# Attention and two expert layers on one core: attention in pairs, one-bank PSUM tiles, another order

## The chip, the cores and the metric

The kernel runs on one core of a Trainium2 chip. The metric is the device time of one execution in microseconds (us), lower is better. The engines are TensorE (PE, with its weight loads as PEld), VectorE (DVE), ScalarE (ACT), GpSimd (POOL) and SyncE (SP), which issues nearly all DMAs.

## What is computed

Attention with memory slots and a local window, then a relu-squared layer of two matrix products, then a gated one:

```python
def _attn_ref(q, k, v, mem_k, mem_v):
    ...
    for c in range(nc):
        ...
        scores = scale * np.matmul(q_c, k_full.transpose(0, 1, 3, 2))
        scores = scores - np.max(scores, axis=-1, keepdims=True)
        a = np.exp(scores)
        a = a / (np.sum(a, axis=-1, keepdims=True) + 1e-09)
        out[:, :, c_start:c_end] = np.matmul(a, v_full)

def _moe_ref(x, w_in, w_out, s, b):
    r = np.maximum(x @ w_in, 0.0)
    return (s * (r * r) + b) @ w_out

def _moe2_ref(x, w_in, w_out):
    h = x @ w_in
    return (h * (1.0 / (1.0 + np.exp(-1.702 * h)))) @ w_out
```

Attention has 4 x 8 heads of 768 positions and 64 columns, in chunks of 32 with 64 keys each (8 of memory, 56 of the window). Its output, 3072 tokens x 512, goes through both layers, whose inner width is 2048.

## The kernel before, in words

**Attention** runs over 24 tiles of 128 tokens (`attend`). For each tile the queries and keys are loaded; PE makes the scores `sc` (L454) as a block of 64 small matmuls of 64x32 by 64x64; DVE takes the maximum and subtracts it (L471, L474); ACT does the exponential; PE transposes the result (`pp`, L487), ACT or DVE copies it to `px`; PE multiplies by the values (`o`, L515, again 64 small matmuls); DVE divides by the sums (L520); PE transposes back (`xx`, L529), and copies and a subtraction split the result into a high and a low part, `xh` and `xl`. Tiles 0 to 3 are parts of their own, and from 4 on two tiles make a part (`parts`); in such a pair, scores, `pp`, `o` and `xx` share a PSUM tile of two banks with the tag "a", or "accA" for those in `SIDE`.

**The products** are made in three passes each: high by high, high by low, low by high. Four of the six blocks of 512 tokens of the first layer go straight: `ph` (L644) in a PSUM bank, the gate on ACT and DVE, then the sums `accA` and `accB` (L677), of four banks in all. The other two blocks, and all of the second layer, go by seven products instead of eight (a Strassen-Winograd scheme, function `wino`, four rounds `s` of eight pairs `p` each). Seven inner products of the first matrix, called A, B, C and D in two parts each (`product`, L1015 to L1017), are summed in the PSUM tiles `ph`, `pb`, `pc` and `pd`. A is copied by ACT into the bank of B, and B into the bank of C (`seed`, L1059), before B's and C's own matmuls begin there. Gates follow (L1027, the first use of another function needs an ACT_TABLE_LOAD), then the splits `oj` and `oq` of their results (L1137, L1140) and seven outer products (`outer_product`, L1166 and L1172), whose results are added and stored by `away` (L1194, L1201). The last one ends with two adds of 512 columns and two stores.

**What sets the order.** Nothing is scheduled by hand: each piece of work is an `op` of the class `Plan`, with the engines that can do it and a planned duration, the ops and buffers that it needs, and a time `need`. `Plan.order` walks a model of the engines and chooses, by a due time `late` that it derives from `need`, which op each engine takes next; a gap `AFTER` is added when another engine has to hear of it. The program is emitted in that order, and each engine runs its own list in order, waiting on semaphores. Ops marked dense are the attention blocks (`sc`, `o`); `SPACE` keeps two of them at least 2.4 us apart. Where PE is planned to be idle for over 0.3 us, filler matmuls `idle` (L1304) on a constant tile `cold` are put in; eight `warm` ones (L301) begin the program.

**PSUM.** `ps_acc` holds the sums, `ps_h` two banks of `ph`, `ps_a` the two banks of attention. `pair` gives the two-bank tiles: a `Banks` of two one-bank tiles for "accB", one tile of two banks for "accA" and "a". Waits between engines are made for tiles.

Of the kernel before, what the change touches and what calls it, by code (L numbers as in the profile page):

```python
# [8 lines left out]
F32 = mybir.dt.float32  # L9
# [23 lines left out]
WARM = 8  # L33
# [12 lines left out]
S_PE = 0.8  # L46
V_PE = 0.8

class Plan:
# [30 lines left out]
    def order(self):  # L80
# [20 lines left out]
        for i in range(len(ops) - 1, -1, -1):  # L101
# [7 lines left out]
            late[i] = self.due.get(i, min(due))  # L109

# [7 lines left out]
        holds, packed = {}, [-9.0]  # L118
# [25 lines left out]
        while left:  # L144
# [29 lines left out]
            if i in self.dense:  # L174
                packed[0] = t
# [40 lines left out]
def attention_moe_moe(ctx: ExitStack, tc: tile.TileContext, q_t, k_w, v_w, w_in1, w_out1, s_b, w_in2, w_out2, out):  # L216
# [13 lines left out]
    ps_a = ctx.enter_context(tc.tile_pool(name="ps_a", bufs=1, space=PS))  # L230
# [55 lines left out]
    def chill(e):  # L286
        cold = pp.tile([P, KT, 512], F32, tag="ys", name="cold")
        T["cold"] = cold[:, 1].bitcast(F32R)
        fill(e, cold[:, 0], 0.0)
        nc.vector.tensor_copy(out=T["cold"], in_=cold[:, 0])  # L290

    plan.tag("r", 1)
    o_cold = op(-999, {"dve": 0.7}, chill, alloc=[("ys", "cold")])
    plan.due[o_cold] = -1000.0
    o_ident = op(-135, {"pool": 0.5}, lambda e: make_identity(nc, ident))
# [8 lines left out]
    op(-999, {"pe": 0.46 * WARM}, warm, after=[o_cold], alloc=[("h", "warm")], uses=["cold"])  # L304


    managers = {"gp": pool_g, "att": pool_a}
# [115 lines left out]
    def bank(name, u):  # L423
        T[name, u] = (ps_acc if u in SIDE else ps_a).tile([P, 2, 512], F32, tag="accA" if u in SIDE else "a", name=name)
        return T[name, u]

    def attend(u):
# [168 lines left out]
        for i in ids if b > 3 else ():  # L596
            z = op(px + 1, {"act": 0.6, "dve": 0.5}, whole(i), after=[bk[i]], uses=[("xx", u), ("px", g)])
            o_xd.append(op(px + 1, {"sp": 0.8}, away(i), after=[z], uses=[("px", g)]))
        for i in ids if b < 4 else ():
            nth = u[i] % 4  # L600
            first = [o_x[u[i] - nth][0]] if nth else []
            z = op(px + 1, {"act": 0.6, "dve": 0.69}, keep(i), after=[bk[i]] + first,
# [10 lines left out]
    def pair(tag, name):  # L613
        if tag == "accB":
# [748 lines left out]
```

## Time and profile before

| | |
|---|---|
| median of 3 runs | 1084.7 us (1083.78 to 1085.21) |
| profiled execution | 1084.78 us, span 1083.0 us |
| PE busy | 1063.8 us, 98% |
| DVE busy | 763.4 us, 70% |
| ACT busy | 598.5 us, 55% |
| TensorE clock granted, mean | 0.998 of full speed |
| DMA | 265.68 MB, mean 245 GB/s |

The span runs from the first to the last instruction on the core; the time of the execution is 1.8 us longer. Busy time is time in which the engine works on something; matmuls overlap, so the time between two starts tells more than a duration. A bracket at the end of a timeline row is the idle time ahead of it and what ended it.

### The profile page before, as it was taken

What the parts mean: (1) busy time and instruction counts of PE and PEld (TensorE: products, weight loads), DVE (VectorE), ACT (ScalarE), POOL (GpSimd) and SP (SyncE); (2) the same over time, 40 slices, a digit from 0 to 9 for tenths busy, and PEclk for the clock granted to TensorE, in tenths of its full rate; (3) what the DMA queues carried; (4) which work ended last, traced back from release to release, by engine and by line L of the source; (5) the groups of instructions that cost most, each with busy time, mean ns of one, the idle gap of its engine ahead of it and who ended that gap; (6) DMA issues with size and microseconds to landing.
All of it is one profiled execution on the core that took longest, in us unless ns stands there. A gap on an engine that the chain in (4) does not pass through costs nothing.

```text
span 1083.0 us, 21691 instructions
## 1 busy us (share of the span) xinstructions
PE 1063.8 (98%) x8588; PEld 908.4 (84%) x8588; DVE 763.4 (70%) x1155; ACT 598.5 (55%) x921; POOL 0.7 (0%) x6
## 2 busy tenths in 40 slices
PE   8899999999999999999999999999999999999998
PEld 6777887778877788788888777999888999888998
DVE  7898986778798658888999554995223985222944
ACT  5668755545666647688744665543355532454432
POOL 0000000000000000000000000000000000000000
PEclk9999999999999999999999999999999999999999
DMA  9988934658699964888978998867656766666662
GB/s 341 313 279 295 304 125 142 229 180 304 212 328 313 371 222 152 308 298 271 326 225 282 340 346 283 262 203 252 195 185 212 235 196 221 193 187 205 196 204 79
DMA packets 151541, 265.68 MB, mean 245 GB/s; under 512 B 14224, under 2 KB 65424, under 8 KB 151440
## 3 DMA queue, kind: packets, MB, share of 16 engines
q1 hardware_dynamic: 151152, 263.77, 72.9%
q8 instruction: 68, 1.11, 0.4%
q10 hardware_dynamic: 288, 0.52, 0.1%
q14 instruction: 33, 0.27, 0.1%
HBM read 190.84 MB, written 73.40 MB: 244 GB/s over the span
## 4 chain that ended last, share of the span: by engine, by line
PE 88%; DMA 2%; ACT 2%; DVE 0%; SPq 0%; issue 0%; DVEq 0%
PE ph L644 14%; PE pc L1166 10%; PE accA L677 7%; PE accB L677 7%; PE pd L1166 6%; PE pb L1166 6%; PE pc L1172 3%; PE pd L1015 3%; PE pd L1017 3%; PE pd L1016 3%; PE ph L1015 3%; PE ph L1017 3%; PE ph L1016 3%; PE pc L1015 2%; PE pc L1017 2%; PE pc L1016 2%
## 5 line engine op out<-in xcount | busy, mean ns | idle before, releaser
L1140 DVE TENSOR_TENSOR oj<-G,oj 128x1024 fp32r<-128x1024 f32 x72 | 87.9, 1222 | 51.3 <-ACT oj L1137 50.8
L1137 ACT CAST oj<-G 128x1024 fp32r<-128x1024 f32 x72 | 75.6, 1051 | 87.5 <-PE pd L1166 28.6
L650 ACT ACTIVATE r<-ph 128x512 f32<-128x512 f32 (+1 forms) x66 | 38.5, 583 | 75.3 <-PE ph L644 68.8
L1137 ACT CAST oq<-G 128x1024 fp32r<-128x1024 f32 x40 | 42.1, 1052 | 51.6 <-PE pc L1166 22.0
L1140 DVE TENSOR_TENSOR oq<-G,oq 128x1024 fp32r<-128x1024 f32 x40 | 48.9, 1222 | 27.3 <-ACT oq L1137 27.3
L1166 PE MATMUL pc<-wih,oj 128*128 128x256 f32 x336 | 62.4, 284 | 0.0
L665 ACT CAST gh<-r 128x512 fp32r<-128x512 f32 (+1 forms) x66 | 40.0, 606 | 37.4 <-PE accB L677 34.9
L1149 DVE TENSOR_TENSOR G<-G 128x1024 f32<-128x1024 f32 x48 | 57.2, 1220 | 0.4
L669 DVE TENSOR_TENSOR gl<-r,gh 128x512 fp32r<-128x512 f32 (+1 forms) x66 | 44.1, 668 | 17.3 <-ACT gh L665 16.7
L368 ACT ACTIVATE u<-st 128x512 f32<-128x512 f32 x64 | 42.6, 670 | 22.8 <-DMA st<-w_in 12.9
L1027 ACT ACTIVATE G<-ys 128x512 f32<-128x512 f32 x64 | 40.6, 634 | 24.9 <-DVE ys L1069 24.4
L1166 PE MATMUL pd<-wih,oj 128*128 128x256 f32 x288 | 53.8, 284 | 0.0
L1166 PEld LDWEIGHTS pc<-wih,oj 128*128 128x128 f32 x336 | 53.3, 192 | 0.0
L1166 PE MATMUL pc<-wil,oj 128*128 128x256 f32 x168 | 47.6, 284 | 0.0
L1166 PEld LDWEIGHTS pd<-wih,oj 128*128 128x128 f32 x288 | 45.9, 192 | 0.0
L1166 PE MATMUL pc<-wih,oq 128*128 128x256 f32 x240 | 45.7, 284 | 0.0
L380 DVE SCALAR_TENSOR_TENSOR u<-u,st 128x512 uint32<-128x512 uint32 x64 | 43.4, 685 | 2.4 <-ACT st L376 1.4
L1166 PE MATMUL pb<-wih,oj 128*128 128x256 f32 x240 | 44.7, 284 | 0.0
L386 DVE SCALAR_TENSOR_TENSOR u<-st,u 128x512 uint32<-128x512 uint32 x64 | 43.5, 686 | 0.5
L376 ACT ACTIVATE st<-st 128x512 uint32<-128x512 uint32 x64 | 42.9, 672 | 0.8 <-DMA st<-w_out 0.7
L657 ACT ACTIVATE r<-r 128x512 f32<-128x512 f32 (+1 forms) x66 | 40.8, 618 | 1.6
L677 PE MATMUL accA<-gh,woh 128*128 128x512 f32 (+1 forms) x132 | 41.5, 390 | 0.0
(253 smaller groups left out, 3011.0 us busy)
## 6 DMA issues: line engine op xcount, KB each, us to landing
wih<-wodh SPq DMA_DIRECT2D x112, 256.0 KB, 2.9
wil<-wodl SPq DMA_DIRECT2D x112, 256.0 KB, 3.4
wih<-wch SPq DMA_DIRECT2D x96, 256.0 KB, 3.5
wil<-wcl SPq DMA_DIRECT2D x96, 256.0 KB, 3.9
st<-w_in SPq DMA_DIRECT2D x32, 512.0 KB, 6.5
st<-w_out SPq DMA_DIRECT2D x32, 512.0 KB, 6.0
k<-k_w SPq DMA_DIRECT2D x24, 512.0 KB, 5.4
v<-v_w SPq DMA_DIRECT2D x24, 512.0 KB, 5.9
```

The costliest lines, as they stand in the source:

```text
L380: nc.vector.scalar_tensor_tensor(out=u, in0=u, scalar=3, in1=T["st", i][:, :, 0], op0=ALU.logical_shift_left, op1=ALU.bitwise_or)
L386: nc.vector.scalar_tensor_tensor(out=u, in0=T["st", i][:, :, 1], scalar=0x80000000, in1=u, op0=ALU.bitwise_and, op1=ALU.bitwise_or)
L644: nc.tensor.matmul(T["ph", i], T[win][x][:, k * P:(k + 1) * P], T["x", m, b][y][:, k, r], start=seen_["hid"] == 1, stop=seen_["hid"] == 3 ...
L669: nc.vector.tensor_tensor(out=gl, in0=T["r", i], in1=gh.bitcast(F32), op=ALU.subtract)
L677: nc.tensor.matmul(T["acc", group, k // 2][:, k % 2][:, r], T[wout][x][:, k * P:k * P + P], T["g", i][y], start=fresh and (x, y) == (0, 0) ...
L1015: nc.tensor.matmul(ph, wh, xh, start=first and i == 0, stop=False, skip_group_check=True)
L1016: nc.tensor.matmul(ph, wh, xl, start=False, stop=False, skip_group_check=True)
L1017: nc.tensor.matmul(ph, wl, xh, start=False, stop=i == 1, skip_group_check=True)
L1137: nc.scalar.copy(out=T[kh], in_=g_of(ty, z))
L1140: nc.vector.tensor_tensor(out=T[kl], in0=g_of(ty, z), in1=T[kh].bitcast(F32), op=ALU.subtract)
L1149: o_raw[out, x] = [op(need, {"dve": 1.22}, lambda e: nc.vector.tensor_tensor(out=g_of(out, z), in0=g_of(a, z), in1=g_of(b, z), op=o), afte ...
L1166: nc.tensor.matmul(a, lt[:, z], rh, start=first and t % 2 == 0 and x == 0, stop=p == HALF - 1 and x == 2, skip_group_check=True)
```

## The change

- **Pairs and form.** The planner no longer keeps dense blocks apart (`SPACE` is gone). It counts 0.09 us for going into the form of the attention blocks and 0.25 for going out of it, so two blocks can stand one directly behind the other. The copies behind transposes wait for all transposes of the pair. Planned durations are set anew (`S_PE`, `V_PE`, `AFTER`, copies, gates).
- **One bank for each PSUM tile.** `pair` gives two one-bank tiles everywhere. Attention has its own two-bank tiles in `ps_x` (tiles of `SIDE`) and `ps_a`; these pools are handed over to `ps_y` and `ps_b` for the sums and the seven products when attention is through with them.
- **Table of shifts.** `SHIFTS`, some 250 entries (first op, number of ops, us), is added to the due times.
- **Start.** `cold` is a memset without a cast; the table of Exp is loaded by an op of its own (`table`); nine warm matmuls.
- **End.** The last outer product of the last round is cut in two halves, one for each bank, and `last` adds and stores bank 1 in two halves of 256 columns and bank 0 in one piece.

```diff
-WARM = 8
+WARM = 9
...
-S_PE = 0.8
-V_PE = 0.8
+S_PE = 0.66
+V_PE = 0.66
+
+SHIFTS = (
+    (3509, 64, 0.24), (1579, 256, -5.54), (408, 256, -2.04), (2922, 1, 0.96), (1298, 16, 5), (690, 1, 18.27),
...
-    AFTER = {"pe": 0.2, "act": 0.05, "dve": 0.05, "pool": 0.2, "sp": 0.1, "aq": 0.1, "none": 0.0}
+    AFTER = {"pe": 0.2, "act": 0.035, "dve": 0.035, "pool": 0.2, "sp": 0.1, "aq": 0.1, "none": 0.0}
...
-    BEAT = 0.24
-    SPACE = 2.4
+    BEAT, COLD, SLOW = 0.24, 6.5, 0.45
+    INTO, OUT_OF = 0.09, 0.25
...
+        shift = [0.0] * len(ops)
+        for at, n, by in SHIFTS:
+            for i in range(at, min(at + n, len(ops))):
+                shift[i] += by
+        late = [x + y for x, y in zip(late, shift)]
...
-            if i in self.dense:
-                t = max(t, packed[0] + self.SPACE)
+            if e == "pe" and (i in self.dense) != packed[0]:
+                t += self.OUT_OF if packed[0] else self.INTO
...
-                if idle > 0.3:
-                    full.append((None, int((idle - 0.3) / self.BEAT)))
+                if clock and idle > 0.3:
+                    full.append((None, int((idle - 0.3) / (self.SLOW if clock < self.COLD else self.BEAT))))
...
-        T[name, u] = (ps_acc if u in SIDE else ps_a).tile([P, 2, 512], F32, tag="accA" if u in SIDE else "a", name=name)
+        T[name, u] = (ps_x if u in SIDE else ps_a).tile([P, 2, 512], F32, tag="s", name=name)
...
-            tc_.append(op(pv, {"act": 0.48, "dve": 0.6}, turned(i), after=[tt[i]], uses=[("pp", u)], **fresh("px")))
+        for i in ids:
+            tc_.append(op(pv, {"act": 0.59, "dve": 0.69}, turned(i), after=list(tt), uses=[("pp", u)], **fresh("px")))
...
     def pair(tag, name):
-        if tag == "accB":
-            return Banks([ps_acc.tile([P, 512], F32, tag=f"{tag}{n}", name=name) for n in range(2)])
-        return (ps_a if tag == "a" else ps_acc).tile([P, 2, 512], F32, tag=tag, name=name)
+        pool = {"accB": ps_acc, "accA": pools.get("ps_y"), "a": pools.get("ps_b")}[tag]
+        return Banks([pool.tile([P, 512], F32, tag=f"{tag}{n}", name=name) for n in range(2)])
...
-            return op(need, {"pe": 1.36}, fn, after=after + ready[x] + [o_in[p, n]],
+            return op(need, {"pe": 1.38}, fn, after=after + ready[x] + [o_in[p, n]] + o_late,
...
+        def last(n, b, part, need, after, end):
+            held = ("turn", s) + BANKS[n]
+            lo, hi = (part, part + 1) if b else (0, 2)
+            z = slice(256 * lo, 256 * hi)
+
+            def fn(e):
+                nc.vector.tensor_tensor(out=spot(b)[:, z], in0=T[held][:, b][:, z], in1=spot(b)[:, z], op=ALU.add)
...
+            d = op(need, {"dve": 0.42 if b else 0.69}, fn, after=[end] + after, uses=[tmp, held])
+            o = op(need, {"sp": 0.37 if b else 0.73}, store, after=[d], uses=[tmp])
...
+                    if s == len(SEVEN) - 1 and n == 2 and p == HALF - 1:
+                        prev = [outer_product(n, p, here + 8 * p + only, key, d, prev + wait, only) for only in range(2)]
...
+    def swap(e):
+        follow("att", "late", bufs=1, side="right")(e)
+        follow("ps_a", "ps_b", bufs=1, space=PS, side="right")(e)
+
+    o_late = [op(-1, {"none": 0.0}, swap, after=stage_ops)]
```

Three places of PE's list show what moves. In these rows the number behind a name tells tiles apart, and `32x64 x32` is one attention block. The first is the startup, tiles 2 and 3; before:

```order
L454 MATMUL sc_506<-k_272,qe_352 32x64 x32
L487 MATMUL pp_546<-ident_137,qe_352 128x128 x4
L1304 MATMUL idle_155<-cold_149 128x512
L515 MATMUL o_565<-v_396,px_556 32x64 x32
L1304 MATMUL idle_155<-cold_149 128x512 x2
L529 MATMUL xx_610<-ident_137,px_556 128x128 x4
L487 MATMUL pp_620<-ident_137,qe_352 128x128 x4
L1304 MATMUL idle_155<-cold_149 128x512 x2
L515 MATMUL o_638<-v_396,px_556 32x64 x32
L1304 MATMUL idle_155<-cold_149 128x512 x2
L529 MATMUL xx_680<-ident_137,px_556 128x128 x4
L1304 MATMUL idle_155<-cold_149 128x512 x2
```

In the change:

```order
L511 MATMUL sc_444<-k_267,qe_340 32x64 x32
L511 MATMUL sc_480<-k_267,qe_340 32x64 x32
L701 MATMUL ph_434<-xl0_401,wih_425 128x256 x4
L701 MATMUL ph_434<-xh0_400,wil_426 128x256 x4
L1393 MATMUL idle_183<-cold_152 128x512 x3
L544 MATMUL pp_544<-ident_140,qe_340 128x128 x4
L544 MATMUL pp_558<-ident_140,qe_340 128x128 x4
L1393 MATMUL idle_183<-cold_152 128x512
L572 MATMUL o_570<-v_382,px_563 32x64 x32
L572 MATMUL o_608<-v_382,px_563 32x64 x32
L1393 MATMUL idle_183<-cold_152 128x512
L586 MATMUL xx_650<-ident_140,px_563 128x128 x4
```

The two tiles ran one behind the other from the transposes on, and now run step by step together.

The second is a pair of tiles in the middle of attention, among the sums of the first layer; before:

```order
L677 MATMUL accB_2609<-gh_2930,wol_1952 128x512
L454 MATMUL sc_3018<-k_2744,qe_2811 32x64 x32
L644 MATMUL ph_3054<-xh1_2585,wih_421 128x512 x4
L644 MATMUL ph_3054<-xl1_2586,wih_421 128x512 x4
L454 MATMUL sc_3018<-k_2744,qe_2811 32x64 x32
L644 MATMUL ph_3054<-xh1_2585,wil_422 128x512 x4
L677 MATMUL accA_2605<-gh_2984,woh_2010 128x512
```

In the change (the scores of the same pair, tiles 12 and 13):

```order
L734 MATMUL accB_2602<-gh_2889,wol_1953 128x512
L734 MATMUL accB_2603<-gh_2889,wol_1953 128x512
L511 MATMUL sc_2995<-k_2725,qe_2790 32x64 x64
L734 MATMUL accA_2598<-gh_2943,woh_2035 128x512
L734 MATMUL accA_2599<-gh_2943,woh_2035 128x512
```

The two blocks of scores had eight expert matmuls of 512 columns between them, and now stand directly behind one another (`x64`).

The third is the second round of seven products, sixth pair; `pc_7481` is the two-bank tile of B and D before, `pd_7464` is one bank of C. Before:

```order
L1015 MATMUL pc_7481<-xl1_6294,wih_7427 128x512
L1016 MATMUL pc_7481<-xl1_6294,wih_7427 128x512
L1017 MATMUL pc_7481<-xl1_6294,wil_7428 128x512
L1015 MATMUL pc_7481<-xl0_6398,wih_7423 128x512
L1016 MATMUL pc_7481<-xl0_6398,wih_7423 128x512
L1017 MATMUL pc_7481<-xl0_6398,wil_7424 128x512
L1015 MATMUL pc_7481<-xl0_6398,wih_7423 128x512
L1016 MATMUL pc_7481<-xl0_6398,wih_7423 128x512
L1017 MATMUL pc_7481<-xl0_6398,wil_7424 128x512
L1015 MATMUL pd_7464<-xh0_6397,wih_7427 128x512
L1016 MATMUL pd_7464<-xh0_6397,wih_7427 128x512
L1017 MATMUL pd_7464<-xh0_6397,wil_7428 128x512
```

In the change (`pc_7524` is the bank of B, `pc_7525` that of D):

```order
L1072 MATMUL pc_7525<-xl0_6356,wih_7433 128x512
L1073 MATMUL pc_7525<-xl0_6356,wih_7433 128x512
L1074 MATMUL pc_7525<-xl0_6356,wil_7434 128x512
L1072 MATMUL pc_7524<-xl1_6307,wih_7438 128x512
L1073 MATMUL pc_7524<-xl1_6307,wih_7438 128x512
L1074 MATMUL pc_7524<-xl1_6307,wil_7439 128x512
L1072 MATMUL pc_7524<-xl1_6307,wih_7438 128x512
L1073 MATMUL pc_7524<-xl1_6307,wih_7438 128x512
L1074 MATMUL pc_7524<-xl1_6307,wil_7439 128x512
L1072 MATMUL pd_7501<-xs_6322,wih_7374 128x512
L1073 MATMUL pd_7501<-xs_6322,wih_7374 128x512
L1074 MATMUL pd_7501<-xs_6322,wil_7375 128x512
```

Before, six D matmuls stood between the last of B and the first of C, which needs the copy of B; now D stands ahead of B, and a second part of A (on `xs`) behind it.

## Rows read from the trace of the kernel before

**Rows 1.** Page, part 1: busy us of each engine (share), instructions
```profile
PE 1063.8 (98%) x8588; PEld 908.4 (84%) x8588; DVE 763.4 (70%) x1155; ACT 598.5 (55%) x921; POOL 0.7 (0%) x6
```

**Rows 2.** Windows: length; busy PE, PEld, DVE, ACT, POOL; PEclk, DMA share, GB/s
```profile
0.00:37.00 37.00, 29.55 (x612) 22.02 (x613) 26.50 (x54) 19.99 (x36) 0.70 (x6) 0.95 0.92 332
37.00:100.00 63.00, 62.32 (x797) 50.87 (x797) 56.55 (x99) 46.43 (x81) 0.00 (x0) 1.00 0.91 303
100.00:400.00 300.00, 297.60 (x3278) 239.61 (x3277) 234.94 (x408) 175.94 (x277) 0.00 (x0) 1.00 0.72 245
400.00:700.00 300.00, 296.03 (x1364) 245.51 (x1363) 239.05 (x368) 194.52 (x310) 0.00 (x0) 1.00 0.83 284
700.00:1078.30 378.30, 378.30 (x2543) 350.40 (x2541) 205.07 (x227) 161.60 (x220) 0.00 (x0) 1.00 0.63 198
```

**Rows 3.** PE groups by form: busy us, mean ns, idle before
```profile
L454 PE MATMUL sc<-k,qe 64*32 64x64 f32 x1536 | 20.6, 224 | 0.1
...
L1304 PE MATMUL idle<-cold 128*128 128x512 f32 x35 | 13.2, 479 | 3.6 <-DVE cold L290 1.9 <-issue 1.7
```

**Rows 4.** PE timeline around two attention blocks: start us, us, operation
```profile
234.53 0.62 PE L677 MATMUL accA<-gh,wol 128*128 128x512 f32 x2
234.98 0.62 PE L677 MATMUL accB<-gh,wol 128*128 128x512 f32 x2
235.53 0.86 PE L454 MATMUL sc<-k,qe 64*32 64x64 f32 x64
236.31 1.21 PE L644 MATMUL ph<-xh,wih 128*128 128x512 f32 x4
237.36 1.09 PE L644 MATMUL ph<-xl,wih 128*128 128x512 f32 x4
238.38 0.86 PE L454 MATMUL sc<-k,qe 64*32 64x64 f32 x64
```

**Rows 5.** PE timeline of the startup, tiles 2 and 3
```profile
21.87 0.86 PE L454 MATMUL sc<-k,qe 64*32 64x64 f32 x64
...
24.04 0.86 PE L454 MATMUL sc<-k,qe 64*32 64x64 f32 x64
...
26.75 0.34 PE L515 MATMUL o<-v,px 64*32 64x64 f32 x12 [0.44 <-ACT px L249]
28.94 0.75 PE L515 MATMUL o<-v,px 64*32 64x64 f32 x52 [1.85 <-issue]
...
33.28 0.98 PE L515 MATMUL o<-v,px 64*32 64x64 f32 x64
...
36.80 0.62 PE L644 MATMUL ph<-xh,wih 128*128 128x256 f32 x3 [0.20 <-ACT xh L249]
```

**Rows 6.** The same view, 30 to 34 us
```profile
30.00:34.00 4.00, 3.86 (x73) 2.82 (x74) 3.24 (x8) 1.71 (x3) 0.00 (x0) 0.57 0.77 274
```

**Rows 7.** Timeline of the end, DVE
```profile
1078.38 1.29 DVE L1194 TENSOR_TENSOR ys<-pc,ys 128x512 f32<-128x512 f32 x2 [6.45 <-PE pc L1166]
```

**Rows 8.** PE's waits, 37 to 400: us in total, times, longest
```profile
PE xx L529 <- DVE px L520: 1.1, 1, 1.1
PE o L515 <- ACT px L249: 1.0, 4, 0.2
```

**Rows 9.** PE's waits, 400 to the end
```profile
PE pd L1015 <- ACT pd L1059: 1.3, 2, 0.7
PE pc L1015 <- ACT pc L1059: 1.2, 1, 1.2
```

**Rows 10.** ACT timeline at two seed copies
```profile
606.29 1.28 ACT L1027 ACT_TABLE_LOAD   x1
...
657.39 0.57 ACT L1059 COPY pd<-pc 128x512 f32<-128x512 f32 x1 [1.09 <-PE pc L1017]
```

**Rows 11.** PE timeline at the same two places
```profile
610.76 0.50 PE L1015 MATMUL pc<-xl,wih 128*128 128x512 f32 x1 [1.18 <-ACT pc L1059]
...
658.02 0.50 PE L1015 MATMUL pd<-xh,wih 128*128 128x512 f32 x1 [0.66 <-ACT pd L1059]
```

More of the change, by code (lines that the diff above doesn't have):

```diff
@@ L286, in chill, with table @@
     def chill(e):
[L287 to L290, printed above, removed]
+        T["cold"] = pp.tile([P, KT, 512], F32, tag="ys", name="cold")[:, 0].bitcast(F32R)
+        fill(e, T["cold"].bitcast(F32), 0.0)
+    def table(e):
+        x = const.tile([P, 1], F32, name="one")
+        nc.scalar.activation(out=x, in_=T["cold"].bitcast(F32)[:, :1], func=AF.Exp)
     plan.tag("r", 1)
-    o_cold = op(-999, {"dve": 0.7}, chill, alloc=[("ys", "cold")])
+    o_cold = op(-999, {"dve": 0.6}, chill, alloc=[("ys", "cold")])
     plan.due[o_cold] = -1000.0
+    plan.due[op(-999, {"act": 1.5}, table, after=[o_cold], uses=["cold"])] = -1000.0
     o_ident = op(-135, {"pool": 0.5}, lambda e: make_identity(nc, ident))
@@ L303, in attention_moe_moe @@
     plan.tag("h", 2)
[L304 to L307 removed]
+    op(-999, {"pe": 0.43 * WARM}, warm, after=[o_cold], alloc=[("h", "warm")], uses=["cold"])
+    managers = {"gp": pool_g, "att": pool_a, "ps_x": pool_x, "ps_a": pool_p}
     def follow(old, new, **kw):
@@ L601, in attend @@
             first = [o_x[u[i] - nth][0]] if nth else []
-            z = op(px + 1, {"act": 0.6, "dve": 0.69}, keep(i), after=[bk[i]] + first,
+            z = op(px + 1, {"act": 0.6, "dve": 0.69}, keep(i), after=bk + first,
                    alloc=[] if nth else [(f"x{HOME[b]}", ("x", 0, b))], uses=[("xx", u)])
@@ L1046, in gates @@
                 b = op(need, {"act": 0.62, "dve": 0.69}, square, after=[b])
-                b = op(need, {"act": 0.73, "dve": 0.54}, affine, after=[b])
+                b = op(need, {"act": 0.815, "dve": 0.54}, affine, after=[b])
             o_g[ty, p] = b
@@ L1150, in sums, with outer_product @@
                 out=g_of(out, z), in0=g_of(a, z), in1=g_of(b, z), op=o), after=after + o_raw[a, x] + o_raw[b, x])]
-        def outer_product(n, p, need, key, d, after):
+        def outer_product(n, p, need, key, d, after, only=None):
             tag, turn = BANKS[n]
@@ L1161, in fn @@
                 if m:
-                    for t in range(4):
+                    for t in range(4) if only is None else range(2 * only, 2 * only + 2):
                         z = slice(t * P, t * P + P)
@@ L1173, in fn @@
                                              stop=p == HALF - 1 and x == 2, skip_group_check=True)
-            return op(need, {"pe": 1.45 if m else 1.36}, fn, after=o_part[n, p // 2] + [d] + after, alloc=taken(tag, held),
+            return op(need, {"pe": 0.72 if only is not None else 1.44 if m else 1.36}, fn, after=o_part[n, p // 2] + [d] + after, alloc=taken(tag, held),
                       uses=[("wp", s, n, p // 2), key + ("h",), key + ("l",), held])
@@ L1254, in wino @@
                 elif n == 2:
-                    away(n, b, b, e, [got["u4", b], got["c22", b]], False, False, b)
+                    if s == len(SEVEN) - 1:
+                        for part in range(b + 1):
+                            last(n, b, part, e, [got["u4", b], got["c22", b]], o_end[n][b])
+                    else:
+                        away(n, b, b, e, [got["u4", b], got["c22", b]], False, False, b)
         for x in range(HALF // 2):
@@ L1258, in wino @@
             free_g[3, x], free_g[1, x] = o_part[5, x] + o_raw[2, x], o_part[2, x]
+    side_ops = []
     for u in parts:
         if u[0] < 8:
+            one = len(plan.ops)
             attend(u)
+            if u in SIDE:
+                side_ops.extend(range(one, len(plan.ops)))
+    o_y_pool = [op(-1, {"none": 0.0}, follow("ps_x", "ps_y", bufs=1, space=PS), after=side_ops)]
     for i in range(2 * NF):
@@ L1279, in attention_moe_moe @@
             attend(u)
-    o_late = [op(-1, {"none": 0.0}, follow("att", "late", bufs=1, side="right"), after=stage_ops)]
+    def swap(e):
+        follow("att", "late", bufs=1, side="right")(e)
+        follow("ps_a", "ps_b", bufs=1, space=PS, side="right")(e)
+    o_late = [op(-1, {"none": 0.0}, swap, after=stage_ops)]
     wo_ops = []
```

30 lines of the change are left out of this document (20 added, 10 removed), and 41 rows, old and new, of the table SHIFTS.

## The prediction, on record before the change was run

> **What bounds the kernel now.** I read the totals first, then idle time by stretch, then the stretches one by one. PE is busy for 1063.8 of 1083.0 us [rows 1], so only two things can shorten the kernel: PE's 19.2 us of idle time, and work that PE does not have to do. By stretch the idle time is 7.45 us before 37 us, 0.68 + 2.40 = 3.08 us in the rest of attention, 3.97 us in 400 to 700, and nothing from 700 to PE's end, where PE is busy 378.30 of 378.30 [rows 2]. The remaining 4.7 us lie at the end. Busy time hides two more losses: 35 fillers of the line `idle` [rows 3], which PE runs where it would wait, and the price of changing form between dense attention blocks and ordinary matmuls. All sums below start from the profiled execution, 1084.78 us, which is 0.1 above the median of the runs.
>
> **Joined attention blocks.** One tile's `sc` or `o` is a block of 64 matmuls on 64x32. The block is 0.86 us long and one matmul 0.224 [rows 3, 4], so 63 starts take 0.86 - 0.224 = 0.64 us, 10 ns each. What a block costs is read from its neighbours. Two 128x512 matmuls take 0.45 (234.53 to 234.98), but the two before the block need 0.55, 0.10 more. The block holds PE for 0.78 (235.53 to 236.31), 0.14 more than its starts. The four matmuls behind it need 1.05 where 4 x 0.227 = 0.91 is due, 0.14 more [rows 4]. Together 0.10 + 0.78 + 0.14 = 1.02 us, of which 0.38 is the change of form there and back. A second block directly behind the first pays only its 0.64 or 0.65, and saves 0.36 to 0.38; I take 0.36. The order of the change has 25 runs of such blocks where the kernel before has 48, so 23 blocks are joined: 20 after the first expert work of tiles 2 and 3, and 3 in the startup, which is counted next. 20 x 0.36 = **7.2 us**. The block is on PE, which bounds, so the gain is all on the path. Bounds: 0 (two tiles change the PSUM address and weights, and no row shows two tiles back to back), and 20 x 0.49 = 9.8, if the 0.11 us by which the next four matmuls (237.36 to 238.38) are over their 0.91 too is a late part of leaving this block, and not the way into the next.
>
> **Startup.** The first `ph` of tiles 2 and 3 comes at 36.80 us [rows 5]. Their chain is `sc` of tile 3 at 24.04, softmax, transposes, `o` of tile 2 at 26.75, which stops after 12 matmuls and goes on at 28.94 with 1.85 us put down to "issue", then `o` of tile 3 only at 33.28, since the two tiles run one behind the other [rows 5]. Between 30 and 34 the granted clock is 0.57, most of it at the lower of the two levels, 1.2 GHz, right behind that hole; it costs (1 - 0.57) x 4 = 1.7 us [rows 6]. The change runs the two tiles, which stay parts of their own with a PSUM tile each, step by step together: `sc` twice in a row, four transposes twice, `o` twice. I work its chain from the same rows. `sc` of tile 2 to its own `o` takes 26.75 - 21.87 = 4.9 now. Together they add the second `sc` (0.64), two more DVE operations (1.29 for two on 128x512 [rows 7]) and four more transposes, about 0.44: 7.3, so `o` at 21.9 + 7.3 = 29.2. From `o` of tile 3 to `ph` it is 36.80 - 33.28 = 3.5 now; with the second `o` 4.1, so `ph` at 33.3. What the second tile adds to that tail on DVE (0.65) and in transposes (0.44) I set against the hole and the queues inside the two stretches, which the two now pass once. Nothing covers the 0.44 here: they are in the 7.3. Against 36.80 the gain is **3.5 us**. Bounds: 0 (the fetch of instructions stalls again, and DVE work of the experts stands between the steps) to 5 (the 1.85 and the 1.7 both go, and 1.4 of queues).
>
> **Waits in the rest of attention.** The 3.08 us consist of `xx` waiting for DVE's normalizing (1.1, one time), `o` waiting for ACT's copies (1.0, four times) and smaller ones [rows 8]. Each also lengthens the first matmul behind it by some 0.11 us (worked out with the next part), so that 8 of them make 4.0. The planner's corrected durations (the copy of a transpose at 0.59 instead of 0.48 on ACT) are those errors which let it place `o` too early. From tile 4 on the copies now wait for all eight transposes of a pair, 0.44 us later for the first; expert matmuls lie in between there and cover it, and without them it would cost 0.44 twice in each of 10 pairs. I take **2.5 us**, bounds -1 and 4.
>
> **Seven products.** The idle time of 400 to 700 is products waiting for seed copies on ACT, `pd` twice and `pc` once among them [rows 9]. Two causes can be seen. At 606.29 an ACT_TABLE_LOAD of 1.28 us stands in ACT's queue ahead of the seed, and PE waits 1.18 us until 610.76 [rows 10, 11]. At 657.39 the copy `pd<-pc` starts 1.09 us after its engine came free, released by PE, and PE then waits 0.66 until 658.02 [rows 10, 11]. The copy reads the bank of product B, but the six D matmuls on the other bank come between (6 x 0.227 = 1.4 us; the order in the part on the change shows them), and B and D are one two-bank tile: the copy waits for the last matmul of both. What the row shows is a wait that is one product too long. The Trainium skill, "PSUM — Partial Sum Buffer", section "PSUM bank collisions raise a hardware error", says that each bank is a RAM of its own and that two engines on different banks do not collide. By it a copy may start once its own bank is done, and the waits of this kind go (0.66 + 0.11 at 658.02); by the row alone it is open whether the tile or the bank is waited for. The sum does not rest on it: the change has one tile for each bank, and orders at least one other product, or an outer product, between B and its C. Also, both seeds of the first pair now stand ahead of the ACT_TABLE_LOAD. With 0.11 behind each wait (0.50 for the first matmul [rows 11], 0.62 - 0.23 = 0.39 for one in a stream [rows 4]) the total is 3.97 + 0.44 = 4.4; I take **4.0**, bounds 0 and 4.4. Behind 700 nothing waits, so nothing can be won there.
>
> **End.** The two last DVE adds of 512 columns take 1.29 us after PE's end [rows 7]. Now bank 1 ends six matmuls earlier and is added in two halves beside PE, and one add of about 0.69 is left: 0.6 less, minus the additional stores on SP. **0.4 us**, bounds 0 and 0.6.
>
> **At nothing:** WARM at 9, the smaller memset and the early table load (their place is before the first data), the new PSUM pools (their handover needs attention to be done, which it is before 400), the shifted due times (they act through the order alone), and fewer fillers (a filler fills a wait, and the wait was counted). If this cover goes, a handover costs up to 1 us.
>
> Sum: 7.2 + 3.5 + 2.5 + 4.0 + 0.4 = 17.6; 1084.8 - 17.6 = **1067.2 us**.
>
> **Rivals.**
> 1. **Preparation becomes the limit (0.22).** From 37 to 100 us DVE is busy for 56.55 of 63 us and DMA at 0.91 of its share [rows 2]. PE that arrives 3.5 us earlier needs its split weights earlier, and these come from DVE. Then startup and attention waits are given back at the next weight, and the products keep half: 7.2 + 0.4 + 2.0 = 9.6, so 1075.2. For it speaks the fullness of DVE; against it that 37 to 100 has only 0.68 us of PE waiting now, and joined blocks take nothing from DVE.
> 2. **The seven products keep their waits (0.08):** the earlier arrival moves the waits elsewhere. 17.6 - 4.0 gives 1071.2. Against it is the distance in the order.
> 3. **Joining saves nothing (0.05):** a change of tile costs as much as a change of form. 1084.8 - 10.4 = 1074.4.
> 4. **Slower by supply of instructions (0.05).** At 28.94 `o` stops for 1.85 us within a block without waiting for another engine [rows 5]. A joined block issues 128 matmuls and as many weight loads (PE and PEld have equal counts, rows 1), 256 instructions in 1.3 us, twice as many as a single one. If each of the 23 stalled for 1.9 us, that is 43.7 - 17.6 = 26.1 more, or 1111. It decides from 10 of 23 stalls on (17.6 / 1.9 = 9.3). For it: the stop at 28.94. Against it: two blocks 2.85 us apart at 235.53 and 238.38 run without a stop [rows 4]. The Trainium skill, "Runtime: NRT & Kernel Launch", section "Instruction fetch mechanics", says that instructions come in blocks of 256, and that crossing from one to the next is mostly hidden. By it no such loss occurs in a stretch without branches; the trace disagrees at 28.94, agrees at 235.53.
>
> **How the numbers follow.** My forecast has 0.60, the rivals 0.22, 0.08, 0.05 and 0.05. Low end: the upper bounds together, 9.8 + 5 + 4 + 4.4 + 0.6 = 23.8, give 1061; 1060 with rounding up of what no row shows. High end: rival 1 with 1 us of room, 1076; rivals 2 and 3 lie inside. A measurement of this kernel tells about 0.2% (2.2 us) from no change. Slower by more than that is rival 4 alone, 0.05; rival 1 in a worse form, where the joints are also waited away, could end within it, 0.03; faster 0.92.
>
> **What would show it.** In the profile after: PE's busy time lower by about 7 us or more through `sc` and `o` runs of x128 matmuls 1.5 us long, and four matmuls of 1.05 behind each pair, not each block; the first `ph` of tiles 2 and 3 at about 33 us, without a hole marked "issue" and without a clock of 0.57; idle time of 37 to 400 under 1 us, and of 400 to 700 under 0.5 us with no seed copy among the waits; 0.7 us of DVE after PE's end. The forecast is wrong if waits for DVE's split weights appear in 40 to 150, if the joined blocks show holes marked "issue" or hold PE for more than 1.45 us, or if PE's idle time stays near 19 us.

## The result, and the profile after

The change takes 1069.97 us (median of 4 runs, 1067.89 to 1071.81) where the kernel before takes 1084.42 in the same comparison: a ratio of 0.9866, with an interval of 0.9846 to 0.9885. The forecast was 1067.2 us, in a range of 1060 to 1076. The profiled execution took 1069.63, with a span of 1067.9, so 15.1 us of span went. The page's first part, against [rows 1]:

```profile
PE 1051.9 (99%) x8575; PEld 906.7 (85%) x8575; DVE 763.7 (72%) x1157; ACT 594.5 (56%) x920; POOL 0.7 (0%) x6
```

PE works 11.9 us less, and its idle time falls from 19.2 to 16.0. The stretches, with the columns of [rows 2]:

```profile
0.00:37.00 37.00, 30.76 (x703) 23.67 (x705) 29.61 (x60) 22.72 (x42) 0.70 (x6) 1.00 0.96 361
37.00:100.00 63.00, 61.47 (x862) 50.91 (x846) 59.27 (x104) 49.84 (x87) 0.00 (x0) 1.00 0.92 317
100.00:400.00 300.00, 295.75 (x3168) 242.99 (x3167) 239.46 (x417) 170.29 (x269) 0.00 (x0) 0.99 0.72 247
400.00:700.00 300.00, 300.00 (x1445) 252.99 (x1444) 243.66 (x365) 195.84 (x310) 0.00 (x0) 1.00 0.83 285
...
30.00:34.00 4.00, 3.48 (x24) 2.84 (x25) 4.00 (x9) 3.54 (x8) 0.00 (x0) 1.00 1.01 371
```

Three things answer to the forecast. In 400 to 700 PE does not wait at all any more (3.97 us before). Between 30 and 34 the clock is at its full level, where [rows 6] had 0.57. In the startup, on PE's timeline, the two tiles go together and the first `ph` of theirs comes at 31.23 instead of 36.80 [rows 5]:

```profile
21.96 1.56 PE L511 MATMUL sc<-k,qe 64*32 64x64 f32 x128 [0.82 <-DMA qe<-q_t]
...
27.23 0.35 PE L572 MATMUL o<-v,px 64*32 64x64 f32 x16
27.73 1.36 PE L572 MATMUL o<-v,px 64*32 64x64 f32 x112 [0.16 <-issue]
...
31.23 0.74 PE L701 MATMUL ph<-xh,wih 128*128 128x256 f32 x4 [0.21 <-ACT xh L303]
```

A fourth thing does not: between 37 and 400 PE is idle for 1.53 + 4.25 = 5.78 us, 2.7 *more* than before. PE's waits in that stretch (us in total, times, longest) say of what:

```profile
PE xx L586 <- issue: 2.6, 1, 2.6
PE sc L511 <- issue: 1.7, 2, 1.2
PE xx L586 <- DVE px L577: 0.5, 2, 0.3
PE o L572 <- DVE px L303: 0.5, 1, 0.5
```

The waits for DVE and ACT of [rows 8] shrank to 1.0 us, but 2.6 + 1.7 and a 0.2 not shown, 4.5 us, are now put down to "issue", time in which PE waits for nothing that the profile shows. It did not occur there before. What one joined block costs is read as in the prediction, from PE's timeline (four matmuls, the joined block, two and two matmuls):

```profile
242.23 1.07 PE L701 MATMUL ph<-xh,wil 128*128 128x512 f32 x4
243.23 1.48 PE L572 MATMUL o<-v,px 64*32 64x64 f32 x128
244.64 0.73 PE L734 MATMUL accA<-gh,woh 128*128 128x512 f32 x2
245.21 0.62 PE L734 MATMUL accB<-gh,woh 128*128 128x512 f32 x2
```

The four matmuls ahead take 1.00 where 0.91 is due (0.09 more), the block 1.41, and two behind it 0.57 for 0.45 (0.12 more): 1.62 us for two tiles, against 2 x 1.02 apart [rows 4]. So a join saves 0.4 where nothing else happens. At the end of the program DVE's adds start ahead of PE's last matmul, where they started behind it before [rows 7]:

```profile
1063.27 1.41 DVE L1276 TENSOR_TENSOR ys<-pc,ys 128x256 f32<-128x256 f32 x3 [4.84 <-PE pc L1223]
```

```profile
1063.67 0.28 PE L1223 MATMUL pc<-wih,oq 128*128 128x256 f32 x1
```

PE ends at 1063.67 + 0.28 = 1063.95, DVE at 1064.68, and the span 3.9 us after PE (4.7 before).

The account of the spans, before minus after: startup 5.6, joins 7.2, idle time in the rest of attention -2.7, seven products 4.5 (3.97 and 0.11 behind each of five waits), end 0.7: 15.3 of 15.1. The 7.2 is not read from this profile, it is the forecast's 20 x 0.36; the other four terms leave 7.0 for it and for whatever else changed in attention.

### The profile page after: what moved, and what is told of

Its sections match the earlier page's. It is cut to its first block, busy times and chain, and to the rows that moved or that the text cites. A ratio compares the mean times of both kernels' runs of the same rounds, so it can differ in the third digit from the quotient of the medians.

```text
span 1067.9 us, 21642 instructions
## 1 busy us (share of the span) xinstructions
PE 1051.9 (99%) x8575; PEld 906.7 (85%) x8575; DVE 763.7 (72%) x1157; ACT 594.5 (56%) x920; POOL 0.7 (0%) x6
## 4 chain that ended last, share of the span: by engine, by line
PE 65%; DMA 2%; DVE 1%; ACT 0%; issue 0%; SPq 0%; DVEq 0%; ACTq 0%
PE pc L1223 10%; PE pd L1223 6%; PE pb L1223 6%; PE pc L1229 3%; PE ph L701 3%; PE ph L1072 3%; PE pd L1072 3%; PE pd L1073 3%; PE ph L1074 3%; PE pd L1074 3%; PE ph L1073 3%; PE pb L1072 2%; PE pb L1073 2%; PE pc L1072 2%; PE pc L1073 2%; PE pb L1074 2%
```

## What the waits marked "issue" are

The longest stands in a pair's transposes, the next within a joined block (PE's timeline):

```profile
296.99 0.38 PE L586 MATMUL xx<-ident,px 128*128 128x128 f32 x2
299.95 1.14 PE L586 MATMUL xx<-ident,px 128*128 128x128 f32 x6 [2.58 <-issue]
...
306.07 0.34 PE L511 MATMUL sc<-k,qe 64*32 64x64 f32 x15 [0.57 <-issue]
```

At 297.12 two of eight transposes are done, and the other six follow at 299.95, with nothing to wait for. Counting what PE had begun by then and by 305.30, at the second stop (windows from 0, the numbers behind the x of PE and PEld):

```profile
0.00:299.90 299.90, 289.34 (x3532) 236.89 (x3533) 251.34 (x446) 187.38 (x305) 0.70 (x6) 1.00 0.75 259
0.00:305.30 305.30, 294.69 (x3659) 241.29 (x3660) 253.59 (x449) 189.55 (x309) 0.70 (x6) 0.99 0.75 261
```

3532 + 3533 = 7065 and 3659 + 3660 = 7319, 254 apart; with a few instructions that this view does not count, the two stops are one block of 256 instructions apart. In between, PE's instruction queue (q8) lands one block; here the DMA queues from 297.5 to 298.6, when DMA is full:

```profile
q1 hardware_dynamic: 109, 0.38, 92.1%
q8 instruction: 1, 0.02, 5.4%
```

PE goes on 1.4 us after that. The 14 profiles of this study have 70 stops of over 0.15 us that nothing else explains, and all follow these two rules: counted over all recorded instructions of PE they stand at 193 over a multiple of 256 (here 449, 961, 1217, 1473, 4801, 7105 and 7361), and each ends 1.16 to 1.59 us after the queue has landed a block. I call such a place a seam. The stop at 28.94 of the kernel before [rows 5], at 961, is one too.

The 14 traces laid together show when a seam stops PE. Take the 31 stretches between two seams from count 1473 to 9409 in each trace, 434 in all. In 109 of them PE needs under 7 us for the 256 instructions (a stop at their end not counted), and 33 of these end in a stop; of the other 325 none does. The next block lands 1.8 us (median) after PE has passed a seam where under 0.7 of DMA's share was taken in the 4 us behind it, and 3.8 us where it was 0.95 or more; 21 of the 33 stops are of the second kind. So two things meet: short instructions leave little time, and the block is late where DMA is full. For the stop at 299.95, PE needed 3.7 us from the seam before, and the block landed 4.8 us after that seam; with the 1.4 us behind the landing, 4.8 + 1.4 - 3.7 = 2.5. From 400 us on the 256 instructions take 15 us or more, and no seam stops PE.

This stop cost more than itself. Right behind it the granted clock is 0.57, mostly its lower level of 1.2 GHz, as [rows 6] had it behind the hole in the startup:

```profile
300.00:304.00 4.00, 4.00 (x14) 3.18 (x13) 2.25 (x3) 1.17 (x2) 0.00 (x0) 0.57 1.02 404
```

That is (1 - 0.57) x 4 = 1.7 us more, so the seams took 4.5 + 1.7 = 6.2 us from the change behind 37 us. Without the 1.7, the 7.0 us left for the joins in the account are 8.7, near the 20 x 0.42 = 8.4 of the block read above.

## Experiments

The theory tested first: joining saves 0.36 us a piece, but a joined block is a whole block of instructions in 1.3 us, and PE runs dry at the seams. The rival: those stops belong to stretches of full DMA, joined or not.

**1. Blocks apart, by the planner's old rule.**

```diff
-            if e == "pe" and (i in self.dense) != packed[0]:
-                t += self.OUT_OF if packed[0] else self.INTO
+            if i in self.dense:
+                t = max(t, packed[0] + self.SPACE)
```

> The change with its rule for dense blocks put back to the old one (at least 2.4 us between two of them), all else as in the change. Theory: a joined block saves 0.36 us of changing form, but its 256 instructions pass in 1.3 us and PE then runs out of instructions, so that 4 to 5 us of waits marked issue came with the 23 joins (4.5 us of them between 37 and 400). Apart, these waits go (under 0.5 us between 37 and 400), PE works 23 x 0.36 = 8.3 us more, and the whole takes some 4 us more than the change: 1072 to 1076. Rival: the issue waits belong to stretches in which DMA is full, joined or not; then some 4 us of them stay, and the time is 1077 to 1080.

Measured: 1086.89 us, ratio 1.0023 (1.0011 to 1.0035), slower than either theory allowed. Waits of PE, from 37 to 400 and from 400 on:

```profile
PE accA L734 <- issue: 2.5, 1, 2.5
...
PE pd L1072 <- ACT pd L1116: 3.3, 2, 2.6
PE ph L1072 <- ACT pb L1116: 1.6, 1, 1.6
```

The stops fell from 4.5 to 2.5 us only, and that one came with no block joined. With another rule the planner makes another order, in which seed copies are late again though all tiles have one bank (6.5 us idle in 400 to 700, 0 in the change), and the table of shifts meets an order other than that of the change. PE is also busy for 9.7 us more, of which the 23 changes of form are 8.3 by the forecast's price. So this run does not price the joins.

**2. Joins alone**, the reverse edit in the kernel before.

> The kernel before with the new rule for dense blocks alone (0.09 and 0.25 us for a change of form in place of the 2.4 us). 20 joins save 20 x 0.36 = 7.2 us. Theory: waits marked issue of 2 to 5 us appear between 37 and 400, where the kernel before has none, each ending 1.3 to 1.6 us after PE's instruction queue has landed a block: 1079 to 1083. Rival (full DMA makes them, not joining): none appear, and the time is 1077.

Measured: 1085.17, ratio 1.0005 (0.9991 to 1.0019), runs from 1081.3 to 1089.7. Joining alone, again in another order of the planner, gains nothing. Its waits from 37 to 400, and on ACT's timeline the copy ahead of the `o` that waited longest:

```profile
PE o L515 <- DVE px L249: 4.4, 1, 4.4
PE xx L529 <- issue: 1.9, 1, 1.9
...
365.85 0.58 ACT L249 COPY px<-pp 128x512 f32<-128x512 f32 x1 [3.64 <-DMA xd<-px]
```

A stop of 1.9 us came, as the theory said, but the larger part of the 7.2 us went into softmax waits: the `o` that waited 4.4 us came behind copies to `px`, the first of which stood on ACT until an earlier store out of the same buffer had landed. Neither theory had this.

**3. One-bank tiles alone**, in the kernel before; each engine's order is unchanged.

```diff
-            return Banks([ps_acc.tile([P, 512], F32, tag=f"{tag}{n}", name=name) for n in range(2)])
-        return (ps_a if tag == "a" else ps_acc).tile([P, 2, 512], F32, tag=tag, name=name)
+        pool = {"accB": ps_acc, "accA": pools.get("ps_y"), "a": pools.get("ps_b")}[tag]
+        return Banks([pool.tile([P, 512], F32, tag=f"{tag}{n}", name=name) for n in range(2)])
```

> The kernel before with one-bank tiles everywhere; each engine's order is the same as before. Theory: the two waits whose copy stands behind D's last matmul on the other bank (at 658.02 and 668.57, 0.66 + 0.11 each) go, the other three (table load, a product directly followed by its user) stay: idle time of 400 to 700 falls from 4.0 to 2.6, the whole to 1083. Rival: the bank frees nothing, since ACT is late by itself: 4.0 stays, 1084.4.

Measured: 1081.24, ratio 0.9968 (0.9955 to 0.9980), 3.5 us less. Waits from 400 on:

```profile
PE ph L1017 <- ACT pb L1061: 0.7, 1, 0.7
PE pd L1017 <- ACT pd L1061: 0.7, 1, 0.7
PE pb L1017 <- ACT ys L1065: 0.6, 1, 0.6
```

Idle time of 400 to 700 is 1.96 us. The waits of 658.02 and 668.57 are gone, and the one behind the table load too; a new one, for `ys`, is short. The other gains are 0.6 at the end and 1.6 in attention (waits of 0.49 at 188.71 and 1.13 at 362.02 are gone), which I did not foresee and whose way was not followed.

**4. Two-bank tiles in the change**, the reverse edit, with each engine's order as in the change.

> The change with two-bank tiles for the sums and products as before; each engine's order is the same as the change's. Theory: the order of the change relies on the banks. At nine places D stands directly ahead of B and at three between B and C on the other bank of the same tile, and each costs PE 0.66 + 0.11 there: 12 x 0.77 = 9.2 us more, 1079, with the idle time of 400 to 1060 near 8. Rival: the order alone removed the waits, and the tiles are of no account: within 1 us of the change, 1070.

Measured: 1080.04, ratio 0.9957 (0.9942 to 0.9971), against 0.9866 for the change: some 10 us more. Waits from 400 on:

```profile
PE pc L1074 <- ACT pc L1118: 2.6, 4, 0.7
PE pb L1074 <- ACT pb L1118: 1.5, 2, 0.8
PE ph L1074 <- ACT ph L1118: 1.3, 2, 0.7
PE pd L1074 <- ACT pd L1118: 0.7, 1, 0.7
```

Nine waits of 0.66 to 0.8 came, of the twelve places, and with 0.11 each make 7.1 us; the end is 4.6 us long again, 0.7 more. Seam stops of 8.0 us in this profile (5.3 in the change's, both with the startup) add 2.7; together 10.5 of the 12.2 by which this profile's span is longer, and the rest is not placed. So without one-bank tiles the order of the change keeps 4.7 of its 14.5 us: the copy waits for the tile, not for the bank it reads.

**5. Blocks apart, in the change's own order.** After the order is made, the second block of a pair is moved behind the next expert piece, or that piece ahead of it, in 19 of 20 pairs behind 37 us.

```diff
+        for a, b, c in zip(pe, pe[1:], pe[2:]):
+            if a in self.dense and b in self.dense and c not in self.dense and starts[a] > 34.0:
...
+                full.insert(y, full.pop(x))
```

> The change with its own order, except that in 19 of the 20 joins behind 37 us the second block is put behind the next expert piece (or that piece ahead of it); DVE's and ACT's order is untouched. This takes the joining alone away, without the planner making another order. Theory: 19 x 0.36 = 6.8 us of changes of form come back, and most of the waits marked issue between 37 and 400 (4 us in the change's profile) go: a net 2 to 4 us, 1072 to 1074. Rival (joining has nothing to do with those waits): 1077, with the waits still there.

Measured: 1075.61, ratio 0.9909 (0.9893 to 0.9925), where the change has 0.9866 and, in experiment 11, 0.9878: 3.4 to 4.7 us more. Experiment 8, which differs from the change in the start only, took 1070.20 in the same comparison, 5.4 less. Waits from 37 to 400:

```profile
PE sc L520 <- issue: 1.3, 2, 0.9
PE pp L553 <- ACT qe L545: 1.2, 2, 0.8
PE xx L595 <- DVE px L586: 1.0, 5, 0.2
```

Stops fell to 1.3 us. So most of them went, and the rival, that joining has nothing to do with them, falls. Joining is not the only way to a stop, as the 2.5 us of experiment 1 show. PE is busy for 1058.5 us, 6.6 more than in the change; the change's busy time holds 1.7 of half clock, which this profile does not have, so the 19 pairs apart cost 8.3, 0.44 each. The net is at the upper end of what was expected or above it, since `pp` and `xx` also wait for softmax steps behind the later second block (1.2 and 1.0 us, where the change has 0 and 0.5). Its four runs lie within 0.6 us, while the change's nine (with those of 11) spread over 7.5, from 1067.9 to 1075.4; but the four of 8, with all joins, lie within 1.2, so it is not shown that the spread comes from the joins.

**6. Seams moved by 96 instructions**, by small warm matmuls at the start.

```diff
-        for _ in range(WARM):
+        for _ in range(3):
             nc.tensor.matmul(w, T["cold"][:, :P], T["cold"], start=True, stop=True)
+        for _ in range(54):
+            nc.tensor.matmul(w[:, :64], T["cold"][:, :P], T["cold"][:, :64], start=True, stop=True)
```

> The change with 54 small warm matmuls of 64 columns and 3 large ones in place of 9 large ones, so that PE issues 96 more instructions (matmuls and weight loads together) ahead of everything else; the order behind is the same. Theory: PE's instructions come in blocks of 256, and PE runs dry at the seam of two blocks when the 256 before it pass faster than a block arrives. The waits marked issue in the change stood at instructions 449, 1217, 1473, 4801, 7105 and 7361, all 193 over a multiple of 256. They now stand at the same counts, that is 96 instructions earlier in the program and in front of other operations; the sum stays between 3 and 9 us, the whole within 3 us of the change (1067 to 1073). Rival (the place decides, by full DMA or by a wait that the profile does not show): the same operations wait as before, the `xx` at 297 among them, at counts 96 higher.

Measured: 1088.04, ratio 1.0030 (1.0018 to 1.0042). A part is the experiment's own fault; PE's timeline:

```profile
2.90 11.56 PE L360 MATMUL warm<-cold 128*128 128x64 f32 x54
...
15.40 1.18 PE L513 MATMUL sc<-k,qe 64*32 64x64 f32 x64
```

The small matmuls took 214 ns each, and the first scores came 8.5 us late. But the stops moved as the theory says: they stand at counts 961, 1985, 3009, 6081, 6849, 8641 and 8897, all 193 over a multiple of 256, in front of other operations, and the `xx` near 297 does not wait any more. Their sum, 13.5 us in this profile, was above the 9 foreseen, and the time is far above the 1073. From one seam to PE's going on at the next took 3.2 us at the shortest here (to 369.26), and 10.1 in experiment 7 (to 65.89). The rival falls, but the price of the phase has to be measured without the late start (12).

**7. No shifts**, `SHIFTS = ()`.

> The change with an empty table of shifts. Theory after the first four runs: what the parts are worth depends on the order that goes with them; without the table the planner's order has seed copies and softmax steps come late, and some 8 us of the gain are lost: 1075 to 1082, with waits for seed copies in 400 to 700 again. Rival: the planner's new costs and the banks carry the gain, and the table is worth 2 us at most: 1070 to 1072.

Measured: 1086.70, ratio 1.0010 (0.9999 to 1.0022). The whole gain is gone. Waits from 37 to 400 and from 400 on:

```profile
PE sc L468 <- issue: 4.9, 2, 3.5
PE pp L501 <- ACT qe L493: 3.1, 2, 2.3
...
PE pb L1029 <- ACT ys L1077: 1.7, 1, 1.7
```

The order that the planner finds with its new rules alone has late softmax steps, seam stops and seed copies. The table picks the order in which banks and joins pay; what it does without them was not run. The rival falls.

**8. The old start**: the cast, eight warm matmuls, no early table load.

```diff
-WARM = 9
+WARM = 8
...
-        fill(e, T["cold"].bitcast(F32), 0.0)
+        fill(e, cold[:, 0], 0.0)
+        nc.vector.tensor_copy(out=T["cold"], in_=cold[:, 0])
```

> The change with the start of before: DVE casts the constant tile, eight warm matmuls, and no early load of the table of Exp; the order of the engines is otherwise the same. Theory: PE begins 0.5 us later, at 1.9, which is hidden, since it waits for k at 6.8; the table load (1.3 us) falls on the first work of ACT behind the first data and costs at most that: 0 to 1.3 us, 1070 to 1071.3. Rival: the start is behind the 1.35 us by which the first expert matmul of tiles 0 and 1 came earlier, and more: 1.5 us or above, 1071.5 or later.

Measured: 1070.20, ratio 0.9860 (0.9843 to 0.9876), as the change. PE begins at 1.91 instead of 1.45, and nothing follows from it.

**9. Three joins taken apart**, chosen by the stops of the change's profile; the edit of 5 with three blocks named.

> The change with only three of its joins taken apart, those at 206.8, 293.6 and 304.1 us, at or behind which PE ran dry at the seams 4801, 7105 and 7361 (3.7 us of waits in the change's profile, 5.7 in that of the run with the old start). Theory: 3 x 0.36 = 1.1 us of form come back, the three waits fall below 1 us together, and the whole gains 2 to 4 us: 1066 to 1068. Rival (the waits move on to the next seams, or the other 16 swaps did the work): no gain, 1070 to 1071.

Measured: 1069.97, ratio 0.9871 (0.9854 to 0.9888), runs from 1067.9 to 1071.3: no gain. Its waits from 37 to 400:

```profile
PE xx L595 <- issue: 1.8, 1, 1.8
PE o L581 <- issue: 1.2, 1, 1.2
```

Two of the three stops are gone, that in the transposes behind the second block stayed at 1.8, and another seam (count 9153) stops `o` for 1.2, as it does in 10 and 11 with all joins in place. The rival is right: this is not a version that beats the change.

**10. The old end**: the last outer product in one piece, one add and store for each bank.

> The change with the end of before: one add of 512 columns and one store for each bank of the last outer product; PE's order is the same. Theory: 0.4 to 0.7 us more behind PE's end, 4.6 us from there to the end of the span, 1070.5. Rival (the last store's landing decides, and its start hardly moves): 0.1 us or nothing.

Measured: 1070.05, ratio 0.9866 (0.9851 to 0.9881). DVE's last adds and PE's last matmul:

```profile
1064.85 1.41 DVE L1251 TENSOR_TENSOR ys<-pc,ys 128x512 f32<-128x512 f32 x2 [4.84 <-PE pc L1223]
```

```profile
1065.25 0.28 PE L1223 MATMUL pc<-wih,oq 128*128 128x256 f32 x1
```

With one add for each bank the first also starts 0.68 us ahead of PE's end (1065.53), and the span ends 3.9 us behind it. The halves are worth nothing; the gain at the end is from the banks, as 3 and 4 show from both sides.

**11. The change again.**

> The change itself, so that it can be set against the three others on the same chip and for a second profile. Theory: 1068 to 1072, with waits at the seams 1217, 1473, 4801, 7105 and 7361 again, of other lengths than in the first profile, since a block's way takes now 4, now 10 us. Rival (the lengths are fixed by the program): the same lengths within 0.2 us.

Measured: 1070.92 (1068.19 to 1075.41), ratio 0.9878 (0.9857 to 0.9898). The profiled execution is the slowest, 1075.41. PE's timeline, to be set beside the change's first:

```profile
301.76 0.81 PE L586 MATMUL xx<-ident,px 128*128 128x128 f32 x6 [3.09 <-issue]
...
307.62 0.34 PE L511 MATMUL sc<-k,qe 64*32 64x64 f32 x15 [1.90 <-issue]
```

Two seams again, with 3.09 for 2.58 and 1.90 for 0.57; those at 1473 and 4801, named beforehand, do not stop PE this time, and one at 9153 has 1.7. The lengths are not fixed by the program. All stops make 9.2 us here, startup included, and 5.3 in the change's first profile, and the clock falls to its lower level, 1.2 GHz, two times instead of one (0.51 in 34.0 to 37.4, 0.57 in 375 to 379). The 3.9 us of stops and the 1.7 of the second fall are 5.6 of the 5.8 us between the two spans.

**12. Seams moved again, with a shorter start.** 51 matmuls of the attention form and 6 warm ones. Each of the 51 is two matmuls for PE (x8674 on its page for x8575), so that the shift was 198 and not 96.

> The shift by 96 instructions again, now by 51 matmuls of the attention blocks' form and 6 warm ones in place of 9, which take no more time than those they replace (in the first try 54 matmuls of 64 columns took 11.6 us and put the first scores 8.5 us back). The order behind is the change's. Theory: the first scores come at 7 us as in the change, the waits marked issue stand in front of the operations of the first try (scores at the counts 961 and 3009, values at 1985, sums at 6081 and 6849), make 8 to 15 us together, and the whole is 1073 to 1081. Rival (the late start made the first try slow, the phase is of no account): 1069 to 1072.

Measured: 1076.34 (1073.38 to 1077.91), ratio 0.9923 (0.9908 to 0.9938), 5.4 us more than the change in the same comparison (11). The start is not free of cost either, as PE's timeline shows: the first scores come at 8.38 instead of 6.98 in 11. Behind it the waits to 37, and from 37 to 400:

```profile
8.38 1.19 PE L515 MATMUL sc<-k,qe 64*32 64x64 f32 x64
...
PE o L576 <- issue: 5.3, 2, 4.5
...
PE accB L738 <- issue: 1.7, 1, 1.7
PE sc L515 <- issue: 1.6, 1, 1.6
```

9.2 us of stops, at counts 449, 705, 1217, 1729 and 7617, again 193 over a multiple of 256; the operations named beforehand were wrong, since the shift was not the one they were worked out for. The stop at 705 alone takes 4.5 us, and the clock is 0.53 behind it (20.5 to 24.1). In the profile of 11 the stops also make 9.2 us, and its execution is the slowest of its five while this one is the fastest of its six, so the two profiles cannot divide the 5.4. It holds the late start, by an estimate from the two first scores 1.4 us, and the phase.

## Why the prediction was right, and where it was wrong

- **The sum** was 17.6 us, and 15.1 of span came; 1067.2 was 2.8 too low. Three terms were too small, the joins held, and one term had the wrong sign. So the total is near in part by luck: startup, products and end gave 2.9 more than taken, joins and the rest of attention together 4.3 instead of 9.7. That the time lies in the range also depends on where the seams fall: moved (12), the same order took 1076.3, some 1.4 of it by the late start.
- **Joins, 7.2 taken:** right as a price (1.62 for two tiles instead of 2.04, and 0.44 for a pair in 5), and the bound of 0, that two tiles behind one another save nothing, is out (rival 3). Not seen was that joining is worth this only in an order made for it (experiment 2: nothing).
- **Startup, 3.5 taken, 5.6 measured:** the step "`sc` of tile 2 to its own `o` takes 4.9 now", with 2.4 us of the second tile's steps on top, was too much: it took 5.3, and `o` came at 27.23, not 29.2. The second tile's steps run beside the first tile's next ones and lie only in small part on the way. DVE's first maximum begins, at 22.84, while the second block of scores still runs (to 23.52), and ACT's first exponential, at 24.93, before DVE's second subtraction has ended (25.44):

```profile
22.84 1.40 DVE L528 TENSOR_REDUCE top<-sc 128x8 f32<-128x512 f32 x2 [0.42 <-PE sc L511]
```

  The hole of 1.85 is a stop of 0.16 now, and the half clock between 30 and 34 went, as the bounds had it. The early table load has no part in it (8). No run takes the joint run of tiles 2 and 3 out alone, so this term is read from the two traces.
- **Waits in the rest of attention, 2.5 taken, -2.7 measured:** the step that failed. The waits named there did shrink (to 1.3 us of idle time), but seam stops of 4.5 us came. The prediction had their mechanism, in rival 4, but priced it as all or nothing: 1.9 us at each of 23 blocks, with a chance of 0.05. It is neither: PE stops at three or four seams behind 37 us, by 0.2 to 3.1 us, where 256 instructions pass in under 7 us and the block is late, and the half clock behind the longest adds 1.7. A term for "some of them" belonged into the sum, and the same rows had its size, 1.85 at 28.94 and the clock of [rows 6].
- **The signs that it named:** one of those against it came, holes marked "issue" within joined blocks, and the idle time of 37 to 400 is 5.8 us, where it named under 1. PE's idle time fell to 16.0, by 3.2; most of the gain is in busy time.
- **Seven products, 4.0 taken, 4.5 measured:** right, with five waits where the sum counted four, and both reasons are needed. Banks alone give 2.0 in this stretch (3), and the order without them costs 7.1 (4). The rule of the Trainium skill, "PSUM — Partial Sum Buffer", section "PSUM bank collisions raise a hardware error", that two engines on different banks do not collide, agrees with the runs: with a tile for each bank the waits of 0.66 at 658.02 and 668.57 are gone.
- **End, 0.4 taken, 0.7 measured,** but for another reason than given: not the halves, but that the add of one bank need not wait for the other (10).
- **Rival 1** (preparation) did not come: with PE 5.6 us earlier, 37 to 100 has 1.53 us of idle time instead of 0.68, not 3.5. **Rival 2** is out.
- The Trainium skill, "Runtime: NRT & Kernel Launch", section "Instruction fetch mechanics", has blocks of 256 instructions, and the seams agree. That crossing them is mostly hidden holds for 400 us and later, where no run shows a stop; between 37 and 400 it holds for 28 of 32 crossings in the change's profile, and the other four stop PE for 4.5 us (6.7 in the profile of 11).

Open is whether full DMA is the cause of late blocks: the two go together in the 14 traces, and the bulk queue takes 92.1% of DMA's share when the block of 297 lands, but a kernel with fewer transfers there was not tried. Open is also by which way the one-bank tiles gained 1.6 us in attention.

## What to carry to other kernels

A wait between engines is made for a tile, so a tile that spans two banks joins two pieces of work that have nothing to do with each other; splitting it cost nothing here and gave 3.5 us in an unchanged order. Parts of a change that is found together are not worth the sum of their parts: the joins alone gave 0, the table's order without the banks lost 10, the rules without the table lost 16. Price the supply of instructions like a transfer: where an engine issues 256 short instructions in about a microsecond, look whether they lie between two seams and whether DMA is full there.

## What the runs showed of the hardware

- All 70 stops of PE without another cause stand at places a multiple of 256 instructions apart, and end 1.2 to 1.6 us after its instruction queue has landed a block; 198 instructions more at the start of the program cost 5.4 us, some 1.4 of it by a late start (12).
- Between counts 1473 and 9409 they came only where 256 instructions passed in under 7 us (33 of 109 times), most of them where DMA was at 0.95 of its share or more.
- The length of a stop varies from run to run (0.57 and 1.90 at one seam). Between two profiles of the change, stops and the half clock behind them make 5.6 of 5.8 us.
- A matmul of 64 columns with a new load of 128 weights took 214 ns in the startup at the full clock (6), where the 64x32 ones of attention need 10 ns each [rows 4].
